# One chunk of z per layer is transposed in blocks by VectorE through DRAM instead of by TensorE

## The chip, the cores and the metric

The kernel runs on one core of a Trainium2 chip. The metric is the device time of one execution in microseconds (us); the median of the runs before is given. TensorE is PE in the rows, VectorE DVE, ScalarE ACT, GpSimd POOL. SP is SyncE, whose one queue (SPq) issues every DMA of this kernel.

## The reference

`x` has 2048 rows of 512 float32. The same four steps run in each of two layers, a Fourier mixing sublayer and an MLP sublayer, each with its own residual:

```
x = x + Re(DFT_seq(DFT_hidden(layernorm(x))))           # products with given DFT matrices
z = layernorm(x)
# the second sublayer, on z:
h  = gelu(layernorm(z) @ w1)                            # z is normalized again inside
hs = concat(shift(g0,+1), shift(g1,-1), shift(g2,+2), shift(g3,-2)) @ w2   # quarters of h, shifted along rows
z1 = z + hs
x  = x + z1 + gelu(layernorm(z1) @ w3) @ w4
```

Weights are shared by both layers. Everything is float32; the kernel computes each product as three products of a high part and a low part (`mm3`): high by high, high by low, low by high.

## The kernel before, in words

Rows are cut into 4 chunks of 512 (`NC`), each of 4 tiles of 128 rows. `S` rows make 16 tiles, held as 8 pairs in SBUF (`xs[0]` to `xs[7]`).

**The Fourier part.** For each output chunk c the kernel runs an x stage (`x_phase`) and then a y stage (`y_phase`), each over 8 pairs k. DFT matrix pieces of 512 KB come from DRAM into 4 buffers (`raw0` to `raw3`), are combined on DVE (lines 254 and 258, `stage_one`), cast to a high part on ACT (line 259) and given a low part on DVE (line 269, `stage_two`). The result lies in one of 4 ring slots (`ring0` to `ring3`), which PE reads. In the y stage one pair of pieces makes two ring items (`by1`, then `by0`); PE does 12 products of 512 columns with each. `prefetch` writes the first half of the next item (line 258) ahead of the low part of the one before it (line 269) in DVE's program order, so a DVE that waits for a piece holds up the low part of an earlier item, too. An engine takes its instructions in program order, SP as well: a DMA issue on SP that waits for a semaphore holds up every DMA issue behind it, the loads of pieces (line 234, `issue_dma`) among them.

**After the last y stage of a layer** come four groups of products with the hidden DFT matrix (`hid`, in the order of `HORDER`, both at the end of the main loop), which finish chunk 3. Their left operands are `rr` (high and low parts made by `run_late`). Then `by_pairs` starts with the first products of w1 (`shifted`), whose right operand is z of chunk 0, transposed: `zt[0]`, with 512 columns on 4 blocks of 128 partitions.

**How z becomes zt before.** Chunk 0 of each layer: in the y stage of the last chunk, `rows(xs[..], x1d, ..)` brings x of tiles 0 to 5 back from DRAM (the table `BACK`, by y step k), ACT normalizes tiles 0 to 3 at k = 4 and 5 into `tmp[:, 0:4]`, and during the `hid` groups 0 and 2 `turn_now` transposes two tiles at a time on PE (line 609), with ACT casting the high part out of PSUM (line 614) and DVE forming the low part (line 615). The other chunks go another way: DVE turns 32 x 32 blocks of a tile (`turn_one`, line 603), four DMAs write the blocks to DRAM (`turn_out`, line 625, 256 KB each, in runs of 512 bytes), one DMA of 1 MB reads them back in order (`turn_in`, line 630), and `z_highs` and `z_lows` split them.

**The MLP part of layer 0** is done in two pairs of chunks. At the end of the first pair the sums z3 of chunks 2 and 3 come from DRAM (`b_in`, line 766), beside loads of w4 (`w4_load`, line 903). In the second pair `work(p)` lists what DVE, ACT and SP do between the products; in its last round p it also splits the first GELU rows (`split_of`).

Of the kernel before, what the change touches and what calls it, by code (L numbers as in the profile page):

```python
# [13 lines left out]
P = 128  # L14
# [5 lines left out]
CH = 512  # L20
# [16 lines left out]
X6, X7 = 2, 4  # L37
QW = (0, 1, 0, 1, 0, 2)
HAT = (2, 3, 3, 4, 5, 5, 6, 6)
BACK = {1: (0,), 2: (2,), 6: (4,)}  # L40
HORDER = ((1, 0), (0, 1), (1, 1), (0, 0))


# [1 line left out]
def spectral_mlp_kernel(ctx: ExitStack, tc: tile.TileContext, x, ws, hs, w1, w2, w34, out, out_t):  # L45
# [47 lines left out]
    def both(name, word, *shape):  # L93
        return at(name, word, *shape), at(name + "f", word, *shape, dtype=F32)

    ay_at = [0, AY, H3, H3 + AY] + [(k - 2) * AY for k in range(4, NP)]
    ay, ayf = zip(*(both(f"ay{k}", word, 4, 2, DH) for k, word in enumerate(ay_at)))
    ax, axf = zip(
        *(both(f"ax{k}", 6 * AY + k * AX if k < 2 else XS - 2 * D + (k - 2) * AX, 3, 2, DH) for k in range(NP))
    )  # L100
    zt, ztf = zip(*(both(f"zt{i}", i * ZW, KD, 2, SW) for i in range(2)))
    w12 = [at(f"w12{i}", W12 + i * 4 * CH, 2, 2, CH) for i in range(4)]
    beside = at("beside", XS - 4 * D - 2 * HALO * KD * 2, 4, D, dtype=F32)
    xs = [at(f"xs{i}", XS + i * 2 * D, 2, D, dtype=F32) for i in range(NP)]
    turn2 = at("turn2", H3, KD, CH, dtype=F32)
    spare = at("spare", SPARE, 2, D, dtype=F32)
    (re0, im0), (re1, im1) = ([both(f"rr{i}{h}", RR + (2 * i + h) * 4 * CH, 2, 2, CH) for i in range(2)] for h in range(2))
    rr = [[re0[0], re1[0]], [im0[0], im1[0]]]
# [402 lines left out]
    def y_phase(c, hook):  # L511
        for k, kind in y_order():
            first, last = k == 0, k == NP - 1
            s = stream()
            if kind == "by1":
                hook(k)
                if k == 2:
                    run_late("y")
                if k == 4:
                    add(re0s, re0s, im1s)  # L520
                mm_half(PC, ay[k][:, 2], s[:, 0], first, last)
                mm_half(PD, ay[k][:, 0], s[:, 1], first, last)
                if last:
                    for i in range(2):
                        nc.vector.scalar_tensor_tensor(
                            im0s[:, i], PC[i], -1.0, im1s[:, i], op0=ALU.mult, op1=ALU.subtract
                        )
                    high(im0)
                    for i in range(2):
                        nc.scalar.copy(X1[:, i], PD[i])  # L530
                    add(im1s, re0s, im0s)
            else:
                if k == NP - 2:
                    low(im0)
                mm_half(PB, ay[k][:, 3], s[:, 1], first, last)
                mm_half(PA, ay[k][:, 1], s[:, 0], first, last)
        t = tmp if c < NC - 1 else beside
        for i in range(2):
            nc.scalar.copy(t[:, i], PB[i])
        for i in range(2):  # L540
            nc.scalar.copy(t[:, 2 + i], PA[i])
        late.update(
            {
                "im1-": [lambda: add(im1s, im1s, re1s, ALU.subtract)],
                "re1+": [lambda: add(re1s, re1s, t[:, 0:2]), lambda: high(re1)],
                "im1+": [lambda: add(im1s, im1s, X1), lambda: high(im1)],
                "re1": [lambda: low(re1)],
                "re0+": [lambda: add(re0s, re0s, t[:, 0:2])],
                "im1": [lambda: low(im1)],
                "re0++": [lambda: add(re0s, re0s, t[:, 2:4]), lambda: high(re0)],  # L550
                "re0": [lambda: low(re0)],
            }
        )
        if c < NC - 1:
            for i, names in enumerate((["im1-"], ["re1+"], ["im1+", "re1"], ["re0+", "im1"], ["re0++"], ["re0"])):
                late[i + 1] = [f for n in names for f in late.pop(n)]
# [45 lines left out]
        v = t.rearrange("p d (a q j) -> p d a q j", a=NB, q=TC)[:, :, :, q]  # L602
        nc.vector.transpose(v, blocks_of(u))

    def turn_now(dst, col, q, u):

        ps = mm_bank()
        for d in range(KD):
            nc.tensor.transpose(ps[:, d * P : (d + 1) * P], u[:, d * P : (d + 1) * P], ident)
        v = ps.rearrange("p (d b j) -> p d b j", d=KD, b=NB)  # L610
        hi, lo = (
            dst[:, :, i, col : col + CH].rearrange("p d (b q j) -> p d b q j", b=NB, q=TC)[:, :, :, q] for i in range(2)
        )
        nc.scalar.copy(hi, v)
        nc.vector.tensor_tensor(lo, v, hi.bitcast(F32), op=ALU.subtract)

    def turn_out(t, to=None):

        if to is None:
# [17 lines left out]

    def zt_split(c):
        turn_split(zt[c % 2], ztf[c % 2], HALO)

    def edges(c):

# [168 lines left out]
    def by_pairs(layer, zs, xin, dst):  # L811
# [62 lines left out]
        def lows(*names):  # L874
            return lambda: [low((blk[b], blkf[b])) for b in names]

        def z_highs(c):
            return lambda: [high(z_half(c, i)) for i in range(2)]

        def z_lows(c):  # L880
            return lambda: [low(z_half(c, i)) for i in range(2)]

        def z_half(c, i):
            return [t[c % 2][:, 2 * i : 2 * i + 2, :, HALO : HALO + CH] for t in (zt, ztf)]

        fs = [NF - 1] + list(range(NF - 1))
        order = fs + fs
# [400 lines left out]
        def second_pair():  # L1290
# [38 lines left out]
            def work(p):  # L1329
                end = p == half - 1  # L1330
                todo = {
                    0: [lambda: q4_sums(p), *([lambda: q4_raw(p + 2)] if p + 2 <= half else [])],
                    1: [lambda: xp_norm_in(p - 1)] if p else [],
                    2: [] if end else [lambda: xp_stats(p)],
                    3: [],
                    4: [lambda: q4_lows(p), lambda: q4_keep(p)],
                }
                if p == 1:
                    todo[3].append(lambda: split_of(0))
                if end:  # L1340
                    todo[0] += [lambda: load(0), lambda: load(1)]
                    todo[1].append(lambda: split_of(1))
                    todo[2] += [lambda: load(2), lambda: load(3)]
                    todo[3] += [lambda: split_of(2), lambda: load(4), lambda: load(5)]
                    todo[4].append(lambda: split_of(3))
                return todo

# [72 lines left out]
        for pair in range(NC // 2):  # L1420
# [101 lines left out]
                one()  # L1522

            if pair == 0:
                for c, names in ((2, ("11", "21")), (3, ("12", "22"))):
                    for half, to in enumerate(names):
                        b_in(c, half, to)
                bg += [sum_of("t1", "12", "11"), sum_of("t2", "22", "t1"), sum_of("t3", "22", "12"), sum_of("t4", "21", "t2")]
                bg += [parts(b) for b in ("11", "21", "12", "22", "t2", "t1", "t3", "t4")]
            for i in range(2):  # L1530
                w4_part(acc1, NF - 3 + i, h4[i])
                w4_load()
            drain(c1, acc1)
            for j in range(c1 * TC, c1 * TC + TC, 2):
                rows(xs[j // 2], dst, j, 2, False)
# [16 lines left out]
    for layer in range(LAYERS):  # L1552
# [4 lines left out]
        for c in range(NC):  # L1557
# [81 lines left out]
            def hook(i):  # L1639
                k, odd = divmod(i, 2)  # L1640
                if layer == 0 and c == 1:
                    if i == 1:
                        xp_sums(NP - 1)
                    if i == 2:
                        xp_highs(NP - 1, False)
                    if i == 3:
                        xp_lows(NP - 1, False)
                if c == 0:
                    if layer:
                        for k, first in ((6, X6), (7, X7)):  # L1650
                            for step, f in zip((0, 1, 3, 4, 6), xp_stages):
                                if i == first + step:
                                    f(k)
                    return
                j = (c - 1) * TC
                if i == 4:
                    rows(X1, xin, j, 2, True)
                if i == 9:
                    rows(X1, x1d, j, 2, False)
                if i == 10:  # L1660
                    rows(X1, xin, j + 2, 2, True)

            x_phase(c, hook)

            def hook(k):
                if k == 1 and c:
                    rows(X1, x1d, (c - 1) * TC + 2, 2, False)
                if c == NC - 1:
                    for j in BACK.get(k, ()):
                        rows(xs[j // 2], x1d if j < 12 else xin, j, 2, True)  # L1670
                    if k in (4, 5):
                        for j in (2 * k - 8, 2 * k - 7):
                            zs[j] = tmp[:, j]
                            normed_act(zs[j], xt(j), ln2[j])

            y_phase(c, hook)

# [4 lines left out]
        for i, (ri, dp) in enumerate(HORDER):  # L1682
# [8 lines left out]
                rows(xs[j // 2], x1d, j, 2, True)  # L1691
            if i == 0:
                run_late("re1", "im1+")
                for q in (0, 1):
                    turn_now(zt[0], HALO, q, zs.pop(q))
            if i == 1:
                run_late("re0+", "re0++")
                zs.update(norm_z((4, 5)))
                halo_out(0, zs[4])
            if i == 2:  # L1700
                run_late("re0")
                for q in (2, 3):
                    turn_now(zt[0], HALO, q, zs.pop(q))
                zs.update(norm_z((6, 7)))
                halo_in(0)
        by_pairs(layer, zs, xin, out if last_layer else x2d)
# [57 lines left out]
```

## Time and profile before

| | us |
|---|---|
| median of 3 runs (1436.72 to 1437.32) | 1437.03 |
| the profiled execution's own time | 1435.9 |
| its span, first to last instruction | 1433.8 |
| PE busy | 1426.3 (99%) |
| DVE busy | 1143.4 (80%) |
| ACT busy | 726.4 (51%) |
| POOL busy | 80.3 (6%) |

The granted clock is 1.00 in the whole span. The chain that ended last is 96% PE. The DMA queue of SP moved 296.83 MB and was busy for 62.3% of 16 engines' span. An idle engine costs nothing unless PE waits for it; the times of single instructions show which of them do.

### The profile page before, as it was taken

What the parts mean: (1) busy time and instruction counts of PE and PEld (TensorE: products, weight loads), DVE (VectorE), ACT (ScalarE), POOL (GpSimd) and SP (SyncE); (2) the same over time, 40 slices, a digit from 0 to 9 for tenths busy, and PEclk for the clock granted to TensorE, in tenths of its full rate; (3) what the DMA queues carried; (4) which work ended last, traced back from release to release, by engine and by line L of the source; (5) the groups of instructions that cost most, each with busy time, mean ns of one, the idle gap of its engine ahead of it and who ended that gap; (6) DMA issues with size and microseconds to landing.
All of it is one profiled execution on the core that took longest, in us unless ns stands there. A gap on an engine that the chain in (4) does not pass through costs nothing.

```text
span 1433.8 us, 17321 instructions
## 1 busy us (share of the span) xinstructions
PE 1426.3 (99%) x6290; PEld 1176.6 (82%) x6290; DVE 1143.4 (80%) x1598; ACT 726.4 (51%) x983; POOL 80.3 (6%) x111
## 2 busy tenths in 40 slices
PE   9999999999999999999999999999999999999998
PEld 7888888888888888888887888888888888888887
DVE  7876997897969888767889979979888698637585
ACT  5563454454565755435554544544445676433352
POOL 2100000000002000000000000000000020000000
PEclk9999999999999999999999999999999999999999
DMA  7326656657554858959746566565665468656594
GB/s 250 132 89 206 205 177 198 211 163 245 197 160 118 281 219 319 374 200 328 237 163 203 164 193 192 188 218 178 194 233 189 133 158 312 207 195 259 169 311 144
DMA packets 131533, 297.93 MB, mean 208 GB/s; under 512 B 15212, under 2 KB 56940, under 8 KB 128248
## 3 DMA queue, kind: packets, MB, share of 16 engines
q1 hardware_dynamic: 131448, 296.83, 62.3%
q8 instruction: 49, 0.80, 0.2%
q14 instruction: 36, 0.29, 0.1%
HBM read 244.08 MB, written 52.72 MB: 207 GB/s over the span
## 4 chain that ended last, share of the span: by engine, by line
PE 96%; DVE 2%; DMA 1%; issue 0%; ACT 0%; POOL 0%; DVEq 0%; ACTq 0%; POOLq 0%; SPq 0%
PE psd L306 11%; PE psd L307 11%; PE psd L308 11%; PE psa L306 9%; PE psa L307 9%; PE psa L308 9%; PE psc L306 6%; PE psc L307 6%; PE psc L308 6%; PE psb L308 6%; PE psb L307 6%; PE psb L306 6%; DMA w4s<-w4c 1%; DMA w4r<-w4a 1%; DVE ring L269 0%
## 5 line engine op out<-in xcount | busy, mean ns | idle before, releaser
L252 ACT CAST ring<-raw 128x1024 fp32r<-128x1024 f32 x127 | 133.1, 1053 | 100.6 <-PE psd L308 47.4
L269 DVE TENSOR_TENSOR ring<-raw,ring 128x1024 fp32r<-128x1024 f32 (+1 forms) x128 | 154.5, 1211 | 22.6 <-ACT ring L252 22.6
L306 PE MATMUL psd<-ring,rr 128*128 128x512 f32 x208 | 80.9, 389 | 0.0
L307 PE MATMUL psd<-ring,rr 128*128 128x512 f32 x208 | 80.9, 389 | 0.0
L308 PE MATMUL psd<-ring,rr 128*128 128x512 f32 x208 | 80.9, 389 | 0.0
L346 POOL TENSOR_TENSOR rs<-ve,mhalf 128x4 f32<-128x4 f32 x16 | 28.7, 1795 | 609.2 <-DVE nm L345 609.2
L259 ACT CAST ring<-ring0f 128x1024 fp32r<-128x1024 f32 x28 | 29.5, 1054 | 55.1 <-DVE ring0f L258 55.1
L269 DVE TENSOR_TENSOR ring<-ring1f,ring 128x512 fp32r<-128x512 f32 (+1 forms) x56 | 53.2, 950 | 0.8 <-ACT ring L255 0.8
L325 POOL TENSOR_TENSOR rs<-ve,mhalf 128x2 f32<-128x2 f32 (+1 forms) x33 | 29.7, 899 | 396.9 <-DVE nb L324 396.9
L306 PE MATMUL psc<-ring,ay 128*128 128x512 f32 x128 | 49.9, 390 | 0.3 <-ACT rr11f L501 0.3
L307 PE MATMUL psc<-ring,ay 128*128 128x512 f32 x128 | 49.9, 390 | 0.0
L308 PE MATMUL psc<-ring,ay 128*128 128x512 f32 x128 | 49.8, 389 | 0.0
L306 PE MATMUL psb<-ring,ay 128*128 128x512 f32 x128 | 49.8, 389 | 0.0
L307 PE MATMUL psb<-ring,ay 128*128 128x512 f32 x128 | 49.8, 389 | 0.0
L308 PE MATMUL psb<-ring,ay 128*128 128x512 f32 x128 | 49.8, 389 | 0.0
L306 PE MATMUL psd<-ring,ay 128*128 128x512 f32 x126 | 49.0, 389 | 0.0
L308 PE MATMUL psd<-ring,ay 128*128 128x512 f32 x126 | 49.0, 389 | 0.0
L306 PE MATMUL psa<-ring,ay 128*128 128x512 f32 x126 | 49.0, 389 | 0.0
L307 PE MATMUL psa<-ring,ay 128*128 128x512 f32 x126 | 49.0, 389 | 0.0
L308 PE MATMUL psa<-ring,ay 128*128 128x512 f32 x126 | 49.0, 389 | 0.0
L307 PE MATMUL psd<-ring,ay 128*128 128x512 f32 x126 | 49.0, 389 | 0.0
L259 ACT CAST ring<-ring1f 128x1024 fp32r<-128x1024 f32 x28 | 29.6, 1056 | 37.8 <-DVE ring1f L258 37.8
(574 smaller groups left out, 4379.6 us busy)
## 6 DMA issues: line engine op xcount, KB each, us to landing
raw<-in_ws SPq DMA_DIRECT2D x183, 512.0 KB, 4.9
raw<-in_hs SPq DMA_DIRECT2D x56, 512.0 KB, 3.6
w3b<-w3d SPq DMA_DIRECT2D x15, 1792.0 KB, 8.1
w4r<-w4a SPq DMA_DIRECT2D x33, 512.0 KB, 7.5
wq<-w4a SPq DMA_DIRECT2D x22, 512.0 KB, 4.9
w3d<-w3b SPq DMA_DIRECT2D x5, 1792.0 KB, 6.6
x1d<-tmp SPq DMA_DIRECT2D x12, 512.0 KB, 7.8
xs<-x1d SPq DMA_DIRECT2D x12, 512.0 KB, 6.3
```

Of the source, the lines that this page charges most:

```text
L252: nc.scalar.copy(dest[:, a:b, 0], r[0][:, a:b])
L259: nc.scalar.copy(dest[:, :, 0], lo)
L269: nc.vector.tensor_tensor(lo[:, i], src[:, i], hi[:, i].bitcast(F32), op=ALU.subtract)
L306: nc.tensor.matmul(o, lh, rh, start=first, stop=False, skip_group_check=onto)
L307: nc.tensor.matmul(o, lh, rl, start=False, stop=False, skip_group_check=onto)
L308: nc.tensor.matmul(o, ll, rh, start=False, stop=last, skip_group_check=onto)
L325: nc.gpsimd.tensor_tensor(rs[:, :n], ve[:, :n], mhalf[:, 0, :n], op=ALU.pow)
L346: nc.gpsimd.tensor_tensor(rs, ve, mhalf[:, :, :2], op=ALU.pow)
```

## The change

- `turn_now` goes. Chunk 0 of z takes the way of the others: in the y stage of the last chunk ACT normalizes tiles 0, 1 at k = 1 and tiles 2, 3 at k = 2; DVE turns tiles 0, 1 at k = 2 and tiles 2, 3 at k = 3 (into `turn0`, a new name for room in SBUF that is free then); `turn_out` stands at k = 3, `turn_in` at k = 6. `high` and `low` of the two halves of `zt[0]` are then placed between the `hid` groups 0, 1 and 2.
- x of tiles 0 to 3 is brought back in the x stage of the last chunk (steps 11 and 13), not in its y stage.
- `ay[4]` to `ay[7]` and `ax[0]`, `ax[1]` start 32 words later in SBUF, so that they no longer lie over the end of `zt[0]`.
- In the first step of every y stage the products into `PD` (psd) come ahead of those into `PC` (psc).
- In layer 0 two of the four z3 loads are issued after a w4 load each, at the end of the first pair.
- In the last round of the second pair `split_of(1)` and `split_of(2)` come one place later each, the first from after the product into b5 to after the GELUs of b1 and y, the second behind two more loads.

```diff
-BACK = {1: (0,), 2: (2,), 6: (4,)}
+BACK = {11: 0, 13: 2}
...
-    ay_at = [0, AY, H3, H3 + AY] + [(k - 2) * AY for k in range(4, NP)]
+    ay_at = [0, AY, H3, H3 + AY] + [ZW + (k - 4) * AY for k in range(4, NP)]
...
+    turn0 = at("turn0", EXT, KD, CH, dtype=F32)
...
-                mm_half(PC, ay[k][:, 2], s[:, 0], first, last)
-                mm_half(PD, ay[k][:, 0], s[:, 1], first, last)
+                jobs = (PC, ay[k][:, 2], s[:, 0]), (PD, ay[k][:, 0], s[:, 1])
+                for job in jobs[::-1] if first else jobs:
+                    mm_half(*job, first, last)
...
-    def turn_now(dst, col, q, u):
-
-        ps = mm_bank()
-        for d in range(KD):
-            nc.tensor.transpose(ps[:, d * P : (d + 1) * P], u[:, d * P : (d + 1) * P], ident)
...
-        nc.scalar.copy(hi, v)
-        nc.vector.tensor_tensor(lo, v, hi.bitcast(F32), op=ALU.subtract)
...
-                    todo[1].append(lambda: split_of(1))
-                    todo[2] += [lambda: load(2), lambda: load(3)]
-                    todo[3] += [lambda: split_of(2), lambda: load(4), lambda: load(5)]
+                    todo[2] += [lambda: load(2), lambda: load(3), lambda: split_of(1)]
+                    todo[3] += [lambda: load(4), lambda: load(5), lambda: split_of(2)]
...
-                for c, names in ((2, ("11", "21")), (3, ("12", "22"))):
-                    for half, to in enumerate(names):
-                        b_in(c, half, to)
+                brought = [(c, half, to) for c, names in ((2, ("11", "21")), (3, ("12", "22"))) for half, to in enumerate(names)]
+                for b in brought[: 2 if layer == 0 else 4]:
+                    b_in(*b)
...
+                if layer == 0:
+                    b_in(*brought[2 + i])
...
+                if c == NC - 1 and i in BACK:
+                    rows(xs[BACK[i] // 2], x1d, BACK[i], 2, True)
...
-                    if k in (4, 5):
-                        for j in (2 * k - 8, 2 * k - 7):
+                    if k == 6:
+                        rows(xs[2], x1d, 4, 2, True)
+                    if k in (1, 2):
+                        for j in (2 * k - 2, 2 * k - 1):
                             zs[j] = tmp[:, j]
                             normed_act(zs[j], xt(j), ln2[j])
+                    if k in (2, 3):
+                        for j in (2 * k - 4, 2 * k - 3):
+                            turn_one(turn0, j, zs.pop(j))
+                    if k == 3:
+                        turn_out(turn0)
+                    if k == 6:
+                        turn_in(ztf[0], HALO)
...
             if i == 0:
                 run_late("re1", "im1+")
-                for q in (0, 1):
-                    turn_now(zt[0], HALO, q, zs.pop(q))
+                high(z_half(0, 0))
             if i == 1:
                 run_late("re0+", "re0++")
+                low(z_half(0, 0))
+                high(z_half(0, 1))
...
             if i == 2:
                 run_late("re0")
-                for q in (2, 3):
-                    turn_now(zt[0], HALO, q, zs.pop(q))
+                low(z_half(0, 1))
```

Two places show how the instructions move. SP in the y stage of the last chunk of layer 0, before (`raw` are pieces, `x1d` and `xs` the rows of x):

```order
L225 DMA x1d_78<-tmp_68 128x2x512
L225 DMA xs0_141<-x1d_78 128x2x512
L234 DMA raw0_175<-in_ws 128x1024
L234 DMA raw1_176<-in_ws 128x1024
L225 DMA xs1_142<-x1d_78 128x2x512
L234 DMA raw2_177<-in_ws 128x1024
L234 DMA raw3_178<-in_ws 128x1024
L234 DMA raw0_175<-in_ws 128x1024
L234 DMA raw1_176<-in_ws 128x1024
L234 DMA raw2_177<-in_ws 128x1024
L234 DMA raw3_178<-in_ws 128x1024
L234 DMA raw0_175<-in_hs 128x1024
```

Two loads of `xs` stand here between the loads of pieces. The same stretch of SP in the changed kernel (`zd1<-turn0` are the four writes of `turn_out`):

```order
L226 DMA x1d_78<-tmp_68 128x2x512
L235 DMA raw0_176<-in_ws 128x1024
L235 DMA raw1_177<-in_ws 128x1024
L235 DMA raw2_178<-in_ws 128x1024
L235 DMA raw3_179<-in_ws 128x1024
L615 DMA zd1_80<-turn0_150 32x16x128 x4
L235 DMA raw0_176<-in_ws 128x1024
L235 DMA raw1_177<-in_ws 128x1024
L235 DMA raw2_178<-in_ws 128x1024
L235 DMA raw3_179<-in_ws 128x1024
L235 DMA raw0_176<-in_hs 128x1024
```

The two loads of `xs` have left the stretch, and four writes stand ahead of its last four loads of DFT pieces. DVE in the same y stage, before (`ring..f` is the first half of an item, `ring` its low part, `rr00f` the sum of line 476):

```order
L269 TENSOR_TENSOR ring0_167<-ring0f_168,ring0_167 128x2x512
L258 TENSOR_TENSOR ring2f_172<-raw3_178,raw2_177 128x2x512
L269 TENSOR_TENSOR ring1_169<-ring1f_170,ring1_169 128x2x512
L258 TENSOR_TENSOR ring3f_174<-raw3_178,raw2_177 128x2x512
L269 TENSOR_TENSOR ring2_171<-ring2f_172,ring2_171 128x2x512
L476 TENSOR_TENSOR rr00f_152<-rr00f_152,rr11f_158 128x2x512
L258 TENSOR_TENSOR ring0f_168<-raw1_176,raw0_175 128x2x512
L269 TENSOR_TENSOR ring3_173<-ring3f_174,ring3_173 128x2x512
```

The `ring0f` near the end reads two pieces that have just landed, and the low part of `ring3` stands behind it. The same stretch in the changed kernel (`turn0` are the blocks of z):

```order
L270 TENSOR_TENSOR ring0_168<-ring0f_169,ring0_168 128x2x512
L605 STREAM_TRANSPOSE turn0_150<-tmp_68 128x16x32 x2
L259 TENSOR_TENSOR ring2f_173<-raw3_179,raw2_178 128x2x512
L270 TENSOR_TENSOR ring1_170<-ring1f_171,ring1_170 128x2x512
L259 TENSOR_TENSOR ring3f_175<-raw3_179,raw2_178 128x2x512
L270 TENSOR_TENSOR ring2_172<-ring2f_173,ring2_172 128x2x512
L477 TENSOR_TENSOR rr00f_153<-rr00f_153,rr11f_159 128x2x512
L259 TENSOR_TENSOR ring0f_169<-raw1_177,raw0_176 128x2x512
L270 TENSOR_TENSOR ring3_174<-ring3f_175,ring3_174 128x2x512
```

Two transposes have come in here, as two more have eight rows earlier, ahead of the statistics of y; the pieces that this `ring0f` reads are now the first that SP issues behind the four writes.

## Rows read from the trace of the kernel before

**Rows 1.** Page, part 1: busy us, share of the span, instructions

```profile
PE 1426.3 (99%) x6290; PEld 1176.6 (82%) x6290; DVE 1143.4 (80%) x1598; ACT 726.4 (51%) x983; POOL 80.3 (6%) x111
```

**Rows 2.** Waits of PE, three of six: total us, times, longest us

```profile
PE psd L306 <- DVE rest L476: 0.5, 1, 0.5
PE psc L306 <- ACT rr11f L501: 0.3, 1, 0.3
...
PE psa L306 <- DMA w4r<-w4a: 0.2, 1, 0.2
```

**Rows 3.** Timeline of PE, first transposes: start us, us, engine, line, op, tiles

```profile
393.34 0.39 PE L308 MATMUL psb<-ring,rr 128*128 128x512 f32 x1
393.57 1.03 PE L609 MATMUL psd<-ident,tmp 128*128 128x128 f32 x8
394.36 0.48 PE L306 MATMUL psc<-ring,rr 128*128 128x512 f32 x1
394.68 0.40 PE L307 MATMUL psc<-ring,rr 128*128 128x512 f32 x1
```

**Rows 4.** Timeline of DVE, low part of rr for the second hid group

```profile
392.59 1.22 DVE L437 TENSOR_TENSOR rr<-rr01f,rr 128x1024 fp32r<-128x1024 f32 x1
```

**Rows 5.** Timeline of PE, first product with zt in layer 0

```profile
411.48 0.39 PE L308 MATMUL psb<-ring,rr 128*128 128x512 f32 x1
411.98 0.46 PE L306 MATMUL psd<-zt,w 128*128 128x512 f32 x1
```

**Rows 6.** Timeline of DVE, last y stage of layer 0; waits in brackets

```profile
353.74 1.23 DVE L258 TENSOR_TENSOR ring2f<-raw,raw 128x1024 f32<-128x1024 f32 x1 [1.12 <-DMA raw<-in_ws]
...
358.29 1.28 DVE L340 BATCH_NORM_STATS2 st<-tmp 128x6 f32<-128x512 f32 x2
...
363.51 1.21 DVE L269 TENSOR_TENSOR ring<-ring0f,ring 128x1024 fp32r<-128x1024 f32 x1
364.65 1.21 DVE L258 TENSOR_TENSOR ring2f<-raw,raw 128x1024 f32<-128x1024 f32 x1
...
370.33 1.21 DVE L258 TENSOR_TENSOR ring0f<-raw,raw 128x1024 f32<-128x1024 f32 x1
371.46 1.21 DVE L269 TENSOR_TENSOR ring<-ring3f,ring 128x1024 fp32r<-128x1024 f32 x1
373.89 1.23 DVE L258 TENSOR_TENSOR ring1f<-raw,raw 128x1024 f32<-128x1024 f32 x1 [1.22 <-DMA raw<-in_ws]
```

**Rows 7.** Timeline of PE, first products with the by0 item of k = 5

```profile
374.53 0.39 PE L306 MATMUL psb<-ring,ay 128*128 128x512 f32 x1
374.75 0.39 PE L307 MATMUL psb<-ring,ay 128*128 128x512 f32 x1
```

**Rows 8.** Timeline of DVE, two block transposes of another chunk

```profile
412.95 1.26 DVE L603 STREAM_TRANSPOSE turn<-tmp 128x512 f32<-128x512 f32 x2
```

**Rows 9.** Timeline of SP, issue of pieces for k = 6

```profile
363.62 0.80 SPq L234 DMA_DIRECT2D raw<-in_ws  x2
```

**Rows 10.** Timeline of SP, four block writes and the load after their landing

```profile
414.24 3.12 SPq L625 DMA_DIRECT2D zd<-turn  x4
420.93 0.38 SPq L630 DMA_DIRECT2D zt1f<-zd  x1
```

**Rows 11.** Timeline of SP, a load right behind eight block writes

```profile
457.04 3.11 SPq L625 DMA_DIRECT2D zd<-scr  x4
460.24 4.66 SPq L625 DMA_DIRECT2D z3d<-scr  x4
465.14 1.04 SPq L630 DMA_DIRECT2D zt1f<-zd  x1
```

**Rows 12.** DMA issues at 465.14: xcount, KB each, us to landing

```profile
zt1f<-zd SPq DMA_DIRECT2D x1, 1024.0 KB, 7.9
```

**Rows 13.** DMA issues at 420.93

```profile
zt1f<-zd SPq DMA_DIRECT2D x1, 1024.0 KB, 5.7
```

**Rows 14.** DMA issues at 363.62, the first of the two pieces

```profile
raw<-in_ws SPq DMA_DIRECT2D x1, 512.0 KB, 4.1
```

More of the change, by code (lines that the diff above doesn't have):

```diff
@@ L94, in both @@
         return at(name, word, *shape), at(name + "f", word, *shape, dtype=F32)
-    ay_at = [0, AY, H3, H3 + AY] + [(k - 2) * AY for k in range(4, NP)]
+    ay_at = [0, AY, H3, H3 + AY] + [ZW + (k - 4) * AY for k in range(4, NP)]
     ay, ayf = zip(*(both(f"ay{k}", word, 4, 2, DH) for k, word in enumerate(ay_at)))
     ax, axf = zip(
-        *(both(f"ax{k}", 6 * AY + k * AX if k < 2 else XS - 2 * D + (k - 2) * AX, 3, 2, DH) for k in range(NP))
+        *(both(f"ax{k}", ZW + 4 * AY + k * AX if k < 2 else XS - 2 * D + (k - 2) * AX, 3, 2, DH) for k in range(NP))
     )
@@ L603, in turn_one @@
         nc.vector.transpose(v, blocks_of(u))
-    def turn_now(dst, col, q, u):
-        ps = mm_bank()
-        for d in range(KD):
-            nc.tensor.transpose(ps[:, d * P : (d + 1) * P], u[:, d * P : (d + 1) * P], ident)
[L610 to L613, printed above, removed]
-        nc.scalar.copy(hi, v)
-        nc.vector.tensor_tensor(lo, v, hi.bitcast(F32), op=ALU.subtract)
     def turn_out(t, to=None):
@@ L639, in zt_split, with z_half @@
         turn_split(zt[c % 2], ztf[c % 2], HALO)
+    def z_half(c, i):
+        return [t[c % 2][:, 2 * i : 2 * i + 2, :, HALO : HALO + CH] for t in (zt, ztf)]
     def edges(c):
@@ L875, in lows @@
             return lambda: [low((blk[b], blkf[b])) for b in names]
[L877 to L884, printed above, removed]
+        z_highs, z_lows = (lambda c, f=f: lambda: [f(z_half(c, i)) for i in range(2)] for f in (high, low))
         fs = [NF - 1] + list(range(NF - 1))
@@ L1668, in hook @@
                 if c == NC - 1:
-                    for j in BACK.get(k, ()):
-                        rows(xs[j // 2], x1d if j < 12 else xin, j, 2, True)
-                    if k in (4, 5):
-                        for j in (2 * k - 8, 2 * k - 7):
+                    if k == 6:
+                        rows(xs[2], x1d, 4, 2, True)
+                    if k in (1, 2):
+                        for j in (2 * k - 2, 2 * k - 1):
                             zs[j] = tmp[:, j]
                             normed_act(zs[j], xt(j), ln2[j])
+                    if k in (2, 3):
[5 more added lines that the diff above has]
+                        turn_in(ztf[0], HALO)
             y_phase(c, hook)
```

## The prediction

> **What bounds the kernel now.** I read the page's busy times first. PE is busy for 1426.3 of 1433.8 us [rows 1]: the kernel is PE's own work with hardly a gap, so a change gains only what it takes out of PE or out of a wait of PE, and loses whatever PE comes to wait for. The waits of PE came next. Three of them belong to places that the change touches, 0.5, 0.3 and 0.2 us [rows 2]. Then PE's timeline: a product of 512 columns starts 0.23 us after the one before it (393.34 to 393.57) [rows 3], and that is the pace nearly everywhere. Last came DVE and SP in the y stage of the last chunk, because there the change adds work to both. DVE makes the low part of ring3 for the by0 item of k = 5 from 371.46 and ends it at 372.67 [rows 6]; PE first reads it at 374.75 [rows 7]. DVE's lead is thus 2.1 us, and twice in that stretch (at 353.74 and 373.89) DVE already waits for a piece from DRAM, 1.1 and 1.2 us [rows 6].
>
> **What is taken off PE.** Eight transposes take from 393.57 to 394.36, 0.79 us, and the product behind them 0.32 instead of 0.23 (394.36 to 394.68) [rows 3]. That makes 0.88 us, with four such blocks (two per layer) 3.5 us. The granted clock is 1.00 throughout, so nothing comes or goes by it. The Trainium skill, "TensorE: Matmul & The Clock Gate", Part 4: PE-mode transpose, gives about 275 ns for a transpose within a kernel. By that figure the 32 transposes would be worth 8.8 us, and my sum below would come out 5.3 lower, at +2.3. The row shows a tenth of a microsecond each, and it decides.
>
> The other edits that touch a wait of PE: psd first in y bears on the 0.3 (psc is still being copied out by ACT), the later splits on the 0.5 (DVE sums held up by the splits), the z3 loads behind w4 on the 0.2 [rows 2]. I take all three as gone; with a slow product behind each, as above, that is 1.3 us (bounds 0 and 1.8). The first product with zt starts 0.50 instead of 0.23 us after the one before it [rows 5], in both layers; I count half of that, 0.3. Gain in all: 3.5 + 1.3 + 0.3 = 5.1 us.
>
> **What is added to DVE.** Two block transposes take 1.26 us, and about 1.2 until the next instruction can start [rows 8]. The first pair stands ahead of the statistics (358.29), the second behind the low part that starts at 363.51 [rows 6]. What follows is 2.4 us later: the low part of ring3 would end at 375.1, not at 372.67, and PE wants it at 374.75 [rows 6, 7]. The lead is used up by this alone, for a stall of 0.3 us. Against it, the two loads of xs have left the stretch, and the wait of 1.12 us at 353.74 may shrink by 0 to 1.1; I take 0.35, a third, since the ring slot sets a limit as well. The split of zt[0] is two instructions of double size in place of four on each engine, and the normalizing is the same work earlier, on an ACT that is busy for half of the span [rows 1]: nothing counted.
>
> **What is added to SP and the DMA queue.** This is the term that decides. SP issues the four writes only when the second pair of transposes is done. That pair starts at 364.65 + 1.2 = 365.85 and ends at t0 = 367.1 [rows 6, 8]. Before, SP issued the pieces for k = 6 at 363.62 [rows 9]; now they stand behind the four writes, whose issue takes 3.12 us [rows 10]. They go out at t0 + 3.2 = 370.3, almost 7 us later. When do they land? The two are 1 MB. A load of 1 MB that was issued right behind such writes landed 7.9 us after its issue [rows 11, 12]; the same load issued after the writes had landed took 5.7 [rows 10, 13]. I take the 7.9, because the place is the same: loads queued directly behind block writes. So both pieces are there at 370.3 + 7.9 = 378.2.
>
> DVE's ring0f, 370.33 before, waits for them and starts at 378.3, 8.0 us later; the low part of ring3 stands behind it and ends at 372.67 + 8.0 = 380.65 [rows 6]. PE wants it at 374.75 [rows 7] and has nothing else to do: a stall of 5.9 us, less the 0.35 above, 5.55. Layer 1 has the same order, so 11.1 us for both.
>
> DVE comes out of that stall without a lead. Two operands of the hid groups are made by DVE just in time already: the low part of rr for the second group ends at 393.81 (392.59 + 1.22) [rows 4], and without the transposes PE would begin that group at 393.57 [rows 3]. I count 0.4 us for each of the two places in each layer, 1.6 us (bounds 0 and 3.2).
>
> **Sum.** 11.1 + 1.6 - 5.1 = 7.6 us slower. On the profiled execution's 1435.9 us (span 1433.8) that is 1443.5; the median before lies 1.1 higher, and 1437.03 + 7.6 = 1444.6 us is the prediction. What a measurement of this kernel can tell from no change is about 0.2%, 2.9 us here.
>
> **Rivals.**
>
> B: the loads flow while the writes drain. The Trainium skill, "DMA: Bandwidth & Descriptors", section "Two DMAs through the same engine are not ordered", says that the descriptors of one queue start in order but are pipelined, reads and writes being separate sides of an engine; by that rule the loads' latency would be hidden behind the writes. Rows 11 and 12 speak against it, with 2.2 us more for the load behind writes, though there eight writes had been queued and here only four. In numbers: the pieces land as if alone, 5.7 us after 370.3, at 376.0 [rows 13]; a single piece of 512 KB already takes 4.1 [rows 14], so two are hardly faster. Low part at 378.45, stall 3.7 - 0.35 = 3.35 per layer; 6.7 + 1.6 - 5.1 = +3.2, 1440.2 us, just at the edge of what can be told.
>
> C, the other side: the pieces are never late for PE. Then the four writes cost nothing and the gains stand: 1437.03 - 5.1 = 1431.9 us (1432.5 with 0.3 of DVE's own lateness in each layer). It needs the pieces at 372.7, where ring0f would start on DVE's own account; it decides as soon as SP reaches the four writes by 363.8 instead of 367.1, with loads as in B. For it speaks that before, SP issues the pieces well ahead, and that the y stage has other waits which could absorb some delay; against it that DVE's order puts the second transposes where I put them, and that no load of this size in the rows takes under 4.1 us. If the z path had more room than I see, or the moved xs loads gave DVE its lead back, it would look like this.
>
> D: more is queued than the two pieces. The pieces for k = 7 follow at once, another 1 MB, and if the four loads share the queue evenly, the first two land with the last. From 4.1 us for 512 KB to 5.7 for 1 MB [rows 13, 14] is 1.6 us per piece, so 3.2 us more per layer; +7.6 + 6.4 = +14, 1451 us. The load of 1 MB back into zt at k = 6, ahead of two pieces of the hid matrix, works to the same side. The pieces before landed one after the other and not together, so I hold this unlikely.
>
> **How the numbers follow.** My forecast 0.64, B 0.16, C 0.12, D 0.08. Slower by over 0.2% (above 1439.9): the forecast, D and half of B, 0.80. Within 0.2%: the other half of B, 0.08. Faster: C, 0.12. The forecast's own range is 1441 to 1448: a stall per layer from 4 us, near B, to 7, and 0 to 3.2 for the hid groups. The range that should hold the time 8 times in 10 goes from 1436.5, below B with all its uncertainty, to 1449.5, half way to D; it leaves out C and most of D.
>
> **What would show it.** In the profile after: no products of L609's kind; in each layer one wait of PE of 4.5 to 7 us at psb in y, k = 5, by0, whose releaser is DVE's low part of a ring item; on DVE just before it, a wait of 5 to 6 us of ring0f for a DMA raw<-in_ws; on SP the four writes of turn0 issued at about 367 and the next raw 3 us later. The waits of rows 2 gone. What would make it wrong: no wait of PE in the y stage (C), a DVE wait of only 2 to 3 us (B) or of over 8 (D), or a second stall of more than 1 us at the hid groups.

## The result and the profile after

The changed kernel takes 1453.16 us (median of 5 runs, 1452.81 to 1454.62), the kernel before 1437.03: a ratio of 1.0115, 95% interval 1.010 to 1.013. The prediction said slower by 7.6 us; it is 16.1 us, outside the forecast's range of 1441 to 1448 us and outside the wider one up to 1449.5. The profiled execution after took 1454.25 us with a span of 1452.3, before 1435.9 with 1433.8, so the two profiles below differ by 18.4 us, a little more than the medians.

The page's busy times, and the waits of PE (total us, times, longest us), against [rows 1, 2]; psa to psd are the tiles of PSUM in which PE's products add up:

```profile
PE 1433.5 (99%) x6258; PEld 1177.6 (81%) x6258; DVE 1148.7 (79%) x1602; ACT 727.1 (50%) x979; POOL 78.7 (5%) x111
```

```profile
PE psb L308 <- DVE ring L270: 13.0, 2, 7.4
PE psd L162 <- POOL mhalf L58: 1.4, 1, 1.4
PE psb L423 <- ACT rr L1577: 0.4, 1, 0.4
PE psc L423 <- ACT rr L1577: 0.2, 1, 0.2
```

PE has 32 instructions fewer (the transposes of [rows 3]) and yet is busy for 7.2 us more. The three waits of [rows 2] are gone; the 1.4 us for `mhalf` stands in the kernel before as well. One new wait has come, twice, 13.0 us in all. PE's timeline at the first of the two, against [rows 7]:

```profile
377.30 0.40 PE L307 MATMUL psb<-ring,ay 128*128 128x512 f32 x1
385.10 0.79 PE L308 MATMUL psb<-ring,ay 128*128 128x512 f32 x1 [7.41 <-DVE ring L270]
385.69 0.63 PE L309 MATMUL psb<-ring,ay 128*128 128x512 f32 x1
386.12 0.63 PE L307 MATMUL psb<-ring,ay 128*128 128x512 f32 x1
```

The wait stands at the second product with the by0 item of k = 5, on DVE's low part. DVE, against [rows 6], and SP, against [rows 9, 10]:

```profile
368.19 1.29 DVE L605 STREAM_TRANSPOSE turn<-tmp 128x512 f32<-128x512 f32 x2
...
382.69 1.23 DVE L259 TENSOR_TENSOR ring0f<-raw,raw 128x1024 f32<-128x1024 f32 x1 [7.56 <-DMA raw<-in_ws]
383.83 1.22 DVE L270 TENSOR_TENSOR ring<-ring3f,ring 128x1024 fp32r<-128x1024 f32 x1
```

```profile
369.51 3.37 SPq L615 DMA_DIRECT2D zd<-turn  x4
372.93 3.57 SPq L235 DMA_DIRECT2D raw<-in_ws  x4
```

Read from the bottom: the loads go out at 372.93, behind the four writes; ring0f waits 7.56 us for them; the low part of ring3 (383.83) stands behind ring0f; PE resumes at 385.10. So far it is the chain that the prediction named. Two things it did not name. After the wait the products start 0.43 us apart (385.69 to 386.12) instead of 0.23. The stretches, with PE's busy time and count in the first column after the window and the granted clock behind POOL's:

```profile
340.00:377.00 37.00, 37.00 (x164) 30.50 (x163) 33.91 (x38) 18.82 (x23) 2.23 (x2) 1.00 0.66 193
380.40:390.60 10.20, 5.50 (x13) 4.34 (x14) 7.39 (x7) 3.14 (x3) 0.00 (x0) 0.50 0.29 98
391.00:410.00 19.00, 19.00 (x84) 15.47 (x83) 16.47 (x16) 12.16 (x15) 0.00 (x0) 1.00 0.83 292
1080.00:1097.00 17.00, 17.00 (x75) 13.59 (x74) 15.30 (x21) 6.64 (x7) 2.23 (x2) 1.00 0.53 137
1100.60:1107.40 6.80, 3.90 (x9) 3.13 (x10) 6.10 (x6) 2.25 (x3) 0.00 (x0) 0.50 0.25 99
```

The granted clock is 0.50 (1.2 GHz) from within each wait until some microseconds behind it. In the first, 13 products fill the 5.5 us that PE is busy; at 0.227 us each (in the kernel before the 13th product after the one at 175.06 starts at 178.01) they would take 2.95, so 2.55 us are lost. In the second, 9 products in 3.9 us: 1.86 lost. Together 4.4 us.

The other thing lies far from the change's stage. The same 30 us of chunk work, first the kernel before and then the changed one, PE's count in the first bracket:

```profile
270.00:300.00 30.00, 30.00 (x134) 24.82 (x133) 27.39 (x28) 16.02 (x20) 0.00 (x0) 1.00 0.48 162
```

```profile
270.00:300.00 30.00, 30.00 (x130) 24.31 (x129) 26.49 (x27) 16.24 (x20) 0.00 (x0) 1.00 0.52 173
```

PE is busy throughout in both, at a granted clock of 1.00, and has 130 products in the stretch instead of 134 (a product that overlaps an edge is counted in). Which ones are slow shows when products are grouped by their operands, here in the changed kernel from 140 to 240 us (xcount | busy us, mean ns of one):

```profile
L308 PE MATMUL psd<-ring,rr 128*128 128x512 f32 x35 | 13.6, 389 | 0.0
...
L308 PE MATMUL psd<-ring,ay 128*128 128x512 f32 x16 | 6.3, 392 | 0.0
...
L308 PE MATMUL psb<-ring,ax 128*128 128x512 f32 x16 | 6.2, 390 | 0.0
```

All of these are 389 in the kernel before. Those with ay and ax are slower, those with rr are not, and of ay and ax the change has moved ay4 to ay7, ax0 and ax1 by 32 words, 128 bytes.

### The profile page after: what moved, and what is told of

The parts are those of the page before. It is cut to its first block, busy times and chain, and to the rows that moved or that the text cites. A ratio compares the mean times of both kernels' runs of the same rounds, so it can differ in the third digit from the quotient of the medians.

```text
span 1452.3 us, 17275 instructions
## 1 busy us (share of the span) xinstructions
PE 1433.5 (99%) x6258; PEld 1177.6 (81%) x6258; DVE 1148.7 (79%) x1602; ACT 727.1 (50%) x979; POOL 78.7 (5%) x111
## 4 chain that ended last, share of the span: by engine, by line
PE 93%; DVE 4%; DMA 2%; SPq 1%; issue 0%; ACT 0%; POOL 0%; DVEq 0%; ACTq 0%; POOLq 0%
PE psd L307 10%; PE psd L309 10%; PE psd L308 10%; PE psa L307 8%; PE psa L309 8%; PE psa L308 8%; PE psb L308 6%; PE psc L308 6%; PE psc L307 6%; PE psc L309 6%; PE psb L309 6%; PE psb L307 6%; DMA raw<-in_ws 2%; DVE ring L270 1%; SPq L615 0%
## 5 line engine op out<-in xcount | busy, mean ns | idle before, releaser
L308 PE MATMUL psb<-ring,ay 128*128 128x512 f32 x128 | 51.5, 402 | 13.0 <-DVE ring L270 13.0
L309 PE MATMUL psb<-ring,ay 128*128 128x512 f32 x128 | 51.1, 400 | 0.0
L307 PE MATMUL psb<-ring,ay 128*128 128x512 f32 x128 | 50.6, 396 | 0.0
L307 PE MATMUL psa<-ring,ay 128*128 128x512 f32 x126 | 50.3, 399 | 0.0
L309 PE MATMUL psa<-ring,ay 128*128 128x512 f32 x126 | 50.1, 397 | 0.0
L308 PE MATMUL psa<-ring,ay 128*128 128x512 f32 x126 | 50.0, 397 | 0.0
```

The source lines that it names most:

```text
L307: nc.tensor.matmul(o, lh, rh, start=first, stop=False, skip_group_check=onto)
L308: nc.tensor.matmul(o, lh, rl, start=False, stop=False, skip_group_check=onto)
L309: nc.tensor.matmul(o, ll, rh, start=False, stop=last, skip_group_check=onto)
```

## The experiments

**Theory.** Three things make the kernel slower, and the gains that were counted stand against them: the stall that the prediction named (T: the four writes on SP ahead of the loads make it), a low clock that follows the stall, and the moved addresses (S). Rivals: DVE's transposes alone make the stall (U); the slow products come from the other edits or the traffic; the low clock has a cause of its own.

**The addresses alone (e_shift32).** The kernel before with two lines of the change:

```
+    ay_at = [0, AY, H3, H3 + AY] + [ZW + (k - 4) * AY for k in range(4, NP)]
+        *(both(f"ax{k}", ZW + 4 * AY + k * AX if k < 2 else ..., 3, 2, DH) for k in range(NP))
```

> The kernel before with nothing but the new addresses of ay4 to ay7, ax0 and ax1 (32 words, 128 bytes, further on). Theory S (the products whose left operand lies at a shifted address run 0.2315 instead of 0.2267 us apart, wherever they stand): +5.9 us, 1442.9 us (1442.0 to 1443.8), with the small excess per product on exactly these tiles, as in the changed kernel. Rival (those products are slowed by what the other edits do, the psd order or the traffic of the turned chunk): no change, 1437.0 us, and all products of ay and ax 0.2267 us apart.

Measured: 1443.88 us against 1437.25, +6.6 (ratio 1.003 to 1.006). Its profile has 131 products from 270 to 300 us. One y stage shows which tiles are slow: from 150 to 170 us PE works with ay0 to ay3, from 172 to 192 us with ay4 to ay7.

```profile
150.00:170.00 20.00, 20.00 (x90) 16.57 (x89) 19.00 (x23) 9.67 (x11) 2.23 (x2) 1.00 0.68 227
172.00:192.00 20.00, 20.00 (x88) 16.22 (x87) 17.96 (x18) 9.55 (x11) 0.00 (x0) 1.00 0.52 180
```

The kernel before has 90 in the second stretch, too:

```profile
172.00:192.00 20.00, 20.00 (x90) 16.57 (x89) 17.95 (x18) 10.45 (x13) 0.00 (x0) 1.00 0.44 160
```

The 132 products with ay4 to ay7, ax0 and ax1 start from 171.42 to 202.09 here, 0.232 us apart; those ahead of them and behind them are 0.227 apart. Four chunks in two layers have 132 such products each, so an estimate from these starts is 6 us in all. S holds: two lines that move no work cost about as much as the prediction's whole sum.

**The change without the addresses (e_noshift).** The same two lines are undone in the changed kernel.

> The changed kernel with the old addresses of ay4 to ay7, ax0 and ax1. Theory S: 1453.2 - 5.9 = 1447.3 us (1446.3 to 1448.3); the two stalls at psb in y, k = 5 (7.4 and 5.6 us) and the stretches at a granted clock of 0.5 behind them stay. Rival (the pace of the products has another cause): 1453.2 us.

Measured: 1448.13 us, 5.0 under the changed kernel, with 134 products from 270 to 300 us. The stall stays, and so does the clock:

```profile
PE psb L308 <- DVE ring L270: 11.1, 2, 5.6
```

```profile
377.00:383.70 6.70, 3.31 (x8) 2.64 (x9) 5.32 (x5) 2.09 (x2) 0.00 (x0) 0.50 0.37 141
1093.70:1100.50 6.80, 6.09 (x14) 4.79 (x15) 6.28 (x6) 2.75 (x3) 0.00 (x0) 0.50 0.17 51
```

Here the stall is 11.1 us, and 22 products take 9.4 us where they would take 5.0, another 4.4.

**The writes behind the loads (e_later, e_later_ns).** The four writes are issued at k = 5, behind the last loads of y, and the load of zt0 at k = 7.

```
-                    if k == 3:
+                    if k == 5:
                         turn_out(turn0)
-                    if k == 6:
+                    if k == 7:
                         turn_in(ztf[0], HALO)
```

With the moved addresses kept:

> The changed kernel, shifted addresses kept, with turn_out in the hook of k = 5 instead of k = 3 (so behind the last four loads of y on SP) and turn_in at k = 7 instead of 6; the transposes on DVE stay where they are. Theory T (the four block writes on SP ahead of the piece loads make the stall, and the low clock follows the stall): both stalls and both stretches at 0.5 go, 13.0 + 0.7 + 4.4 = 18.1 us less, 1435.1 us (1434 to 1437). Rival U (the four block transposes, 5 us of DVE ahead of ring work, make the stall): most of it stays, over 1447 us. Rival V (the writes now stand ahead of the loads of the hid groups and stall those instead): a wait of some 5 us per layer at the first hid product, about 1445 us. If the low clock has a cause of its own, it stays near 390 us without a stall, and the time is 1439.5 us.

and with the old ones:

> The changed kernel with both: the old addresses, and turn_out at k = 5, turn_in at k = 7. Theories T and S together: 1453.2 - 18.1 - 5.9 = 1429.2 us (1428 to 1431.9), faster than the kernel before by the 5 to 8 us that the prediction counted as gain and what else went. If T or S fails, as in the runs that undo one of them alone: 1435 with S alone failing, 1447 with T failing.

Measured: 1440.28 and 1435.92 us, 12.9 and 17.2 under the changed kernel where 18.1 and 24.0 were expected. The stall at psb is gone and the granted clock is 1.00 throughout the products of both, so T holds, U falls as the cause of the stall, and the low clock does not come without it. The 4.4 us between the two runs are the cost of the addresses once more. But both times lie above their ranges, and the second kernel is no more than level with the one before (ratio 0.998 to 1.000): smaller waits have come. Its waits of PE, and DVE at that place:

```profile
PE psc L308 <- DVE ring L270: 1.8, 2, 1.1
...
PE psb L307 <- DMA w3b<-w3d: 1.1, 1, 1.1
PE psc L309 <- DVE rr L438: 0.7, 4, 0.2
```

```profile
365.47 1.29 DVE L605 STREAM_TRANSPOSE turn<-tmp 128x512 f32<-128x512 f32 x2
...
373.46 1.22 DVE L270 TENSOR_TENSOR ring<-ring3f,ring 128x1024 fp32r<-128x1024 f32 x1
376.13 1.23 DVE L259 TENSOR_TENSOR ring1f<-raw,raw 128x1024 f32<-128x1024 f32 x1 [1.45 <-DMA raw<-in_ws]
```

DVE is 2.0 us later than in [rows 6] at the low part of ring3 (373.46 for 371.46) and 2.2 at ring1f (376.13 for 373.89): two pairs of transposes. PE then waits one product group later, at k = 6. The three waits make 3.6 us of the 6.7 by which the second run lies above its expectation; what of the rest is the slow start behind each wait was not taken apart.

**One write ahead, three behind (e_first_write).** To part SP's wait for the transposes from the writes themselves: the old addresses, one write at k = 3, three at k = 5.

```
                     if k == 3:
-                        turn_out(turn0)
+                        turn_out(turn0, n=(0, 1))
+                    if k == 5:
+                        turn_out(turn0, zd[count["turn"] % 2], (1, NB))
```

> The changed kernel with the old addresses (as e_noshift, 1448.1 us), and only the first of turn_out's four block writes at k = 3; the other three follow at k = 5, behind the last loads of y. SP waits for the second pair of transposes as before, but one write instead of four (0.9 us of issue instead of 3.3, 256 KB instead of 1 MB) stands ahead of the loads. Theory Q (the writes' issue and bytes delay the loads): the stall at psb, k = 5, falls from 5.7 us to 0 to 1.5 us per layer, the granted clock stays at 1.0, and the time is 1436 to 1440 us. Theory W (it is SP's wait for the transposes, 2.4 us, that counts): a stall of 3 us or more per layer stays, 1440 to 1444 us.

Measured: 1440.12 us, granted clock 1.00 from 374 to 392 us. The stall falls from 11.1 to 3.0 us for both layers:

```profile
PE psb L308 <- DVE ring L270: 3.0, 2, 1.5
PE psb L307 <- ACT beside L541: 2.2, 2, 1.6
PE psc L308 <- DVE ring L270: 1.4, 2, 0.8
```

So moving three of the four writes away takes 8 of the 11 us (Q, at the upper edge of its ranges: 1.5 us of stall per layer, and a time just past 1440); the first write and SP's wait for the transposes, not parted here, leave 3. The two causes do not simply add up: a later run (e_best3) has all four writes at k = 3 again, but its transposes are done before y, so that SP does not wait for them, and it has no stall. The wait on ACT in the second row nobody had expected; it is taken up below.

**The small edits alone (e_small).** The kernel before with psd first, the z3 loads and the splits later; the first chunk is still turned on PE.

```
+                jobs = (PC, ay[k][:, 2], s[:, 0]), (PD, ay[k][:, 0], s[:, 1])
+                for job in jobs[::-1] if first else jobs:
+                    mm_half(*job, first, last)
...
+                    todo[2] += [lambda: load(2), lambda: load(3), lambda: split_of(1)]
```

> The kernel before with only the small edits: psd first in y's first product, two z3 loads later, the splits one point later; the first chunk is still turned on PE. By the prediction's rows the three waits of 0.5, 0.3 and 0.5 us go and nothing else moves: 1437.25 - 1.3 = 1436.0 us (1435.5 to 1436.5). Rival (the waits come back one product later): 1437.2 us.

Measured: 1435.15 us against 1437.18, -2.0 (ratio 0.9976 to 0.9994). The three waits do go, and the interval of the gain, 0.9 to 3.4 us, holds the 1.3 counted. (The expectation has 0.5 for the third wait where [rows 2] has 0.2; its sum is the prediction's 1.3.) Its profile also shows changes that were not counted: the kernel before waits 0.8 and 0.2 us for ACT at line 422, which is gone, and a wait of 1.0 us for a load of w3b has come.

**The transposes out of the y stage (e_best1, e_best2).** From the version with old addresses and turn_out at k = 5 (e_later_ns): the rows of the chunk are loaded at steps (hooks) 8 and 9 or 11 of the x stage and normed and turned there, where DVE waits; first one pair, then both. The edit for both:

```
+                for at_norm, at_turn, j0 in [(10, 11, 0), (11, 12, 2)]:
+                    if c == NC - 1 and i == at_norm:
...
+                            normed_act(zs[j], xt(j), ln2[j])
+                    if c == NC - 1 and i == at_turn:
...
+                            turn_one(turn0, j, zs.pop(j))
```

> As e_later_ns (old addresses, turn_out at k = 5; 1435.9 us), with the first pair of rows loaded, normed and transposed in the x stage (hooks 8, 10, 11) where DVE waits, and the second pair at k = 2 of y where the first was; so 1.2 us of DVE less lie ahead of the last ring work of y. If DVE's lateness (2.0 to 2.3 us against before) makes the waits left in e_later_ns (0.9 and 1.2 us at psc, k = 6, and 0.35 us four times in the hid groups, 4.2 us with the restarts): half of the lateness goes, and with it most of the waits: 1432.5 us (1431.5 to 1434). If they come from late loads: 1435.9 us.

> As e_best1, with both pairs in the x stage (hooks 10 to 12), so that no transpose is left on DVE in y. If DVE's lateness makes the waits left in e_later_ns, all of them go: 1435.9 - 4.2 = 1431.7 us (1431 to 1433), which is 5.5 us under the kernel before. If they come from late loads: 1435.9 us. If the second pair now delays the first ring work of y: a wait at its first product, 1434 us.

Measured: 1433.67 and 1432.53 us (ratio of the second 0.9955 to 0.998). The wait at psc falls from 1.8 to 0.9 and 0.3 us: that was DVE's lateness, as expected. The four waits of 0.2 us in the hid groups stay, which was not. DVE and SP of the second version suggest why:

```profile
375.16 1.23 DVE L259 TENSOR_TENSOR ring1f<-raw,raw 128x1024 f32<-128x1024 f32 x1 [2.09 <-DMA raw<-in_ws]
```

```profile
368.56 1.44 SPq L235 DMA_DIRECT2D raw<-in_ws  x2
370.05 4.17 SPq L615 DMA_DIRECT2D zd<-turn  x4
```

The writes now stand right behind the last pair of loads, and ring1f waits 2.09 us for it against 1.22 in [rows 6]. That the writes delay these loads fits; the next run tests it.

**The writes back at k = 3, transposes early (e_best3).** In the version above, turn_out at 3 and turn_in at 6 as in the changed kernel; SP no longer waits for a transpose there.

> As e_best2 (old addresses, both pairs of rows turned on DVE in the x stage; 1432.5 us), with turn_out back at k = 3 and turn_in at k = 6, where the changed kernel has them. SP no longer waits for a transpose there, so the four writes go out some 4 us before DVE frees the pieces that the loads behind them need. If it was the writes' time on SP and in the queue just ahead of the loads (e_noshift), or just behind them (e_best2: the last pair lands 1.3 us later than in the kernel before, DVE waits 2.1 us), then here neither happens: the waits at psc, k = 6 (0.2 and 0.5 us) and in the hid groups (four of 0.35 us) go too, 1432.5 - 2.8 = 1429.7 us (1429 to 1431.5). If the place ahead of the loads is bad by itself: the stall at psb, k = 5, is back, over 1436 us.

Measured: 1433.5 us, not 1429.7. The writes do no harm at this place: they go out at 358.46, the loads at 363.98 (363.62 in [rows 9]), ring1f waits 1.17 us again, and no wait at psb with ay is left. Of the four waits for `rr` in the hid groups one of 0.2 us is left. A new one took back the gain, on ACT, the same as in the run with one write ahead. Waits of PE, then ACT and SP:

```profile
PE psb L307 <- ACT beside L541: 2.3, 2, 1.7
```

```profile
388.53 1.06 ACT L253 CAST ring<-raw 128x1024 fp32r<-128x1024 f32 x1 [1.94 <-DMA raw<-in_hs]
389.49 1.06 ACT L541 COPY beside<-psb 128x512 f32<-128x512 f32 x2
```

```profile
379.11 0.42 SPq L620 DMA_DIRECT2D zt0f<-zd  x1
380.00 0.82 SPq L235 DMA_DIRECT2D raw<-in_hs  x2
```

ACT waits for pieces of hs that stand on SP behind the 1 MB load of zt0, and copies psb out late behind that wait.

**The load of zt0 behind the hs pieces (e_best4).** turn_in at k = 7, all else as in the last one.

> As e_best3 (1433.5 us), with turn_in at k = 7 instead of 6, so that the load of zt0 (1 MB) stands behind the four loads of hs on SP and not between them. In e_best3 ACT waits 1.9 us for the second pair of hs pieces and copies psb out late, and PE waits 0.6 and 1.7 us there (psb<-ring,rr in the hid groups), 2.85 us with the restarts. If it is the place of the zt0 load, these two waits go: 1433.5 - 2.9 = 1430.6 us (1430 to 1431.5), 6.3 us under the kernel before. If the hs loads are late because of something else: 1433.5 us.

Measured: 1430.96 us against 1437.27 of the kernel before (ratio 0.9945 to 0.9972), as expected. The wait on ACT is gone:

```profile
PE psd L162 <- POOL mhalf L58: 1.4, 1, 1.4
PE psc L309 <- DVE rr L438: 0.4, 2, 0.2
PE psc L423 <- ACT rr L1577: 0.2, 1, 0.2
PE psb L307 <- DMA w3b<-w3d: 0.2, 1, 0.2
```

This version beats both kernels: 6.3 us under the kernel before and 22 under the changed one, with the same products as the latter.

**What it is about the addresses (e_shift64, e_base32).** The kernel before with the six tiles 256 bytes further on (64 words for 32), and the kernel before with the whole arena, the SBUF block that holds all these tiles, 128 bytes further on. The second edit:

```
-    base = -(-nc.sbuf_base // 32) * 32
+    base = -(-nc.sbuf_base // 32) * 32 + 128
```

> The kernel before with the six tiles 256 bytes further on instead of the 128 of e_shift32 (1443.9 us). If what counts is where a left operand starts within 256 bytes (128 in the kernel before, 0 in the changed one), the products of ay4 to ay7, ax0 and ax1 are 0.2267 us apart again: 1437.2 us. If any move from the old addresses costs: 0.2315 us apart, 1443 us or more.

> The kernel before with every tile of the arena 128 bytes further on, left and right operands alike (and two buffers instead of four for the small statistics tiles, to make room). If the start of the left operand by itself counts: nearly all of the 6,200 products run 0.2315 us apart, +30 us, about 1467 us. If it is how left and right operand lie to each other: all as before, 1437 us.

Measured, one run each: 1436.52 and 1437.45 us. From 270 to 300 us both start 134 products, like the kernel before; here the one with 256 bytes and then the one with the whole arena:

```profile
270.00:300.00 30.00, 30.00 (x134) 24.84 (x133) 27.38 (x29) 16.22 (x20) 0.00 (x0) 1.00 0.48 160
```

```profile
270.00:300.00 30.00, 30.00 (x134) 24.86 (x133) 27.46 (x29) 16.25 (x20) 0.00 (x0) 1.00 0.49 162
```

Moving left and right operands together costs nothing, and moving the left ones by 256 bytes costs nothing; moving only the left ones by 128 does. So in these four layouts it counts how the two operands of a product lie to each other, not where the left one starts.

## Why the prediction was wrong, point by point

**Right: the place and the cause of the stall.** The prediction had "a stall of 5.9 us, less the 0.35 above, 5.55" in each layer, 11.1 for both. The change without its address edit has waits of 5.5 and 5.6, 11.1 in all. Its links are right one by one, so the size is no luck; SP and DVE of that run in layer 0:

```profile
370.18 3.41 SPq L235 DMA_DIRECT2D raw<-in_ws  x4
```

```profile
377.97 1.22 DVE L259 TENSOR_TENSOR ring0f<-raw,raw 128x1024 f32<-128x1024 f32 x1 [5.54 <-DMA raw<-in_ws]
```

The prediction had 370.3 and 378.3. In the changed kernel itself the first wait is 7.4, since its loads took longer (issued at 372.93, used at 382.69); the second is 5.6.

**The rivals.** B let the loads flow while the writes drain, with 3.35 us of stall per layer; the measured waits lie above it even without the moved addresses, and taking three writes out from ahead of the loads took 8 us off. The Trainium skill, "DMA: Bandwidth & Descriptors", section "Two DMAs through the same engine are not ordered", says that descriptors of one queue start in order but are pipelined; here that did not hide the loads behind the writes. D's time, 1451 us, was near, but for another reason than its own: the pairs of pieces did not land together, for ring1f waits for the pair of k = 7 until 385.22, 2.5 us after ring0f got its own.

**The step that failed: "The granted clock is 1.00 throughout, so nothing comes or goes by it."** That was read from the kernel before, and its sum then put the clock at nothing for a kernel that would stand still for over 5 us in each layer. Each of the four long stalls (two in the changed kernel, two without the address edit) ends at 0.50, and 22 products at that pace cost 4.4 us in each of the two kernels. The Trainium skill, "TensorE: Matmul & The Clock Gate", section "HAM oscillation — how this bites in real kernels", tells of a kernel that waits for its DMAs and comes back at half the clock each time; the rows agree, and the sum should have had a term for it.

**The step that is missing: the addresses.** The prediction went through what the diff moves in time and never gave the two lines that move tiles in memory a term. Over all chunks they cost 4.4 us (between e_later and e_later_ns), 5.0 (undone in the changed kernel) and 6.6 (alone in the kernel before); the estimate from the starts is 6.

**Gains: about right.** The 32 transposes are gone; no run takes them out alone, so their 3.5 us stay as read from [rows 3]. The prediction set 275 ns for one transpose against the tenth of a microsecond of its row. Both fit the trace of the kernel before: each lasts 270 to 273 ns (shortest, median and longest below), and they overlap, so that the next starts 0.1 us later; the later start is what counts in the sum.

```profile
L609 PE MATMUL psd<-ident,tmp x16: 270/272/273, 393.6 to 1104.8; 128*128 128x128 f32 x16
```

The waits of [rows 2] are gone, and the small edits alone give 2.0 us (0.9 to 3.4) for the 1.3 counted. The first product with zt starts without a gap in both layers, 0.5 us where 0.3 was counted; layer 0, on PE's timeline, against [rows 5]:

```profile
423.04 0.39 PE L309 MATMUL psb<-ring,rr 128*128 128x512 f32 x1
423.27 0.40 PE L307 MATMUL psd<-zt,w 128*128 128x512 f32 x1
```

The last version, without the stall, the low clock and the moved addresses, is 6.3 us under the kernel before, which fits 3.5, 2.0 and 0.5.

**Hid groups: counted 1.6, measured 0.2** in the changed kernel, one product of layer 1 that starts 0.41 us after the one before it (1120.29 to 1120.70). That the products at half the clock give DVE time to get ahead again is argued, not tested.

**The new sum**, on the profiled executions: 13.0 of stall, 4.4 of low clock, 4.4 to 6.6 of addresses and 0.2 in the hid groups, less 3.5, 2.0 and 0.5: 16.0 to 18.2 us, for a measured 18.4. The prediction's 7.6 plus its two missing terms of 4.4 and 4.4 to 6.6 is 16.4 to 18.6, for a difference of the medians of 16.1. The sizes come from runs that scatter by a microsecond or two, so a closer fit would be chance.

**What stays open.** How the loads' lateness divides between SP's issue of the writes and the writes' place in the DMA queue was not parted further. Why the loads of the changed kernel took 2 us longer in layer 0 than without the moved addresses is not shown, nor why the operands' places matter; no shift other than 128 and 256 bytes was run.

## What to carry to other kernels

A new DMA costs its place: list what stands behind it on its queue and who waits for that. Here the same writes cost 11 us of stall, and 4.4 us of low clock behind it, when they went out just ahead of late loads, and nothing visible 8 us earlier, and a load of 1 MB cost 2.3 us until it stood two places later. A stall of PE as long as these, 5.5 us and more, is to be priced with the products behind it at half the clock. And an edit of addresses is an edit of time: where tiles move, compare the pace of the products that read them, in a stage that the rest of the change does not touch.

## What the hardware showed that was not expected

Products of 512 columns with both operands at the old addresses start 0.227 us apart. With the left operand moved by 128 bytes against the right one, they start 0.232 us apart. With 256 bytes, or with both operands moved by 128, the pace is the old one (134 products in the 30 us where the kernel before has 134, and the moved tiles 130 or 131).

The granted clock fell to 0.50 within all four waits of 5.5 to 7.4 us; it stayed at 1.00 through waits of 1.5 us (e_first_write) and 1.7 us (e_best3). No wait of a length between was measured.
